# A planned attention-and-MLP kernel: head groups outermost in half of the blocks, gelu as one ScalarE batch, MLP work spread out, a new prologue

## The chip, the cores and the metric

The kernel runs on one core of a Trainium2 chip. A core has a matrix engine (TensorE, PE in the profile, with its weight loads as PEld), a vector engine (VectorE, DVE), an activation engine (ScalarE, ACT), a general engine (GpSimd, POOL) and a queue engine for transfers (SyncE, SP). Each works through its own instructions in order; they wait for each other by semaphores. On-chip data lies in SBUF, matmul results in PSUM, which has eight banks of 128 x 512 float32. The metric is the device time of one execution in microseconds.

## The reference, cut to what matters

Two branches share one normalised input, and their sum is added to `x` (2048 tokens, 512 columns).

```python
xn = layernorm(x)                                   # [1, 2048, 512]
# A: attention with 32 heads of 16 columns
qkv = xn @ wqkv;  scores = q @ k.T * 16 ** -0.5     # 32 x 2048 x 2048
a = softmax(scores) @ v;  A = a @ wo
# B: an MLP over the token axis
h = layernorm(xn)
u = gelu(einsum("bsd,sf->bdf", h, w1) + b1)         # tanh form; F = 1376
B = (einsum("bdf,fs->bds", u, w2) + b2).transpose(0, 2, 1)
out = x + A + B
```

The softmax needs 32 x 2048 x 2048 exponentials, about 134 million. They are what the kernel spends most instructions' time on.

## The kernel before, in words

**Tiling.** A block is one group of four heads (interleaved in the partitions) against 512 queries. There are 32 blocks: four query blocks `qb`, and in each eight head groups, named by `T` (0 to 3, a 128-column slice of Q, K and V) and `e_` (0 or 1). Each block has 16 key tiles and two half steps, so 32 *score tiles* of 128 x 1024, and the kernel has 1024 of them, numbered `n`. `blk_of` (L600) turns `n` into block, key tile, `qb`, `T` and `e_`. The query block is the outer loop, so all four slices `T` of K and V must be there within the first eight blocks (n up to 255).

**A score tile's way.** TensorE computes it with two matmuls (L616) into one of three *slots* of two PSUM banks. Then it takes one of two ways. Either ScalarE takes one exponential over 1024 columns (L640). Or VectorE builds a power of two from the bits: one pass from PSUM (L651, `dexp`) writes an int16 pattern that reads as a bfloat16, and three shifted copies of it (L656) are made on VectorE or GpSimd; the four together stand for one exponential. In both ways TensorE multiplies the result by V (L679, `pv`), once for a ScalarE tile, four times for a VectorE tile. V has a 17th column of constants, so the softmax's denominator comes out of the same matmuls. After a block, `task_epilogue` (L865) evacuates the sums (L870), divides and regroups them through small transfers (L907).

**Other work.** `task_qt`, `task_kt`, `task_vt` make the later slices of Q, K and V; `task_ut` makes one of 11 slices of u with 16 matmul steps, adds the bias (L804), and takes gelu by hand: two VectorE steps (L808, L810), a tanh on ScalarE (L812) and a last VectorE step (L814). It writes twice the gelu, and 0.5 at the end makes up for it. `task_fin` makes one of 16 output tiles: 11 steps with w2, then the attention's four steps with `wo`, then the evacuation (L854). All of them accumulate in one PSUM bank, `EX_BANK`, so only one runs at a time. GpSimd makes h from xn in the background (L478).

**Order.** Block 0 is written out by hand: two score tiles, two ScalarE exponentials, then a piece of the remaining prologue (`block0_work`, L594). VectorE takes no score tile there. From n = 32 on, a planner in the kernel's Python program (the `Sched` class and the loop behind L1113) keeps a modelled clock for each engine and appends, one at a time, whichever instruction it finds can start first. The chip only sees the resulting orders. The rules that matter here:

- a background task may start once `n` has reached its release number, and it goes ahead of other TensorE work when its due number comes near (L1017 to L1034);
- a score tile is issued when ScalarE will need one (L1197): `need = sc.free["act"] + EXP_I * ahead - 0.46 - DEAD_SLACK`, where `ahead` is the number of score tiles that wait to be taken. Up to that moment TensorE does `pv` or background work;
- VectorE takes a score tile if fewer than `D_FLY` = 3 of its tiles have shifts left to do and eight buffers are free (L1128).

**Prologue.** The loads of x go out on SP (six of them) and those of wqkv on ScalarE's queue (six). `pro_stage` (L558) pipelines statistics, normalisation, transposes and the first Q, K, V tiles over four token tiles. GpSimd computes one root per tile (L456, L458) behind several memsets (L375 to L400).

Of the kernel before, what the change touches and what calls it, by code (L numbers as in the profile page):

```python
# [9 lines left out]
BF16 = mybir.dt.bfloat16  # L10
# [18 lines left out]
GELU_C = 0.7978845608028654  # L29
GELU_A = 0.044715  # L30
# [16 lines left out]
NPRE = 4  # L47

# [15 lines left out]
D_STEAL = 0.8  # L64
P_KEEP = 4
DEAD_SLACK = 0.1
PORT_SLACK = 0.5
PE_FIT = 0.05

# [22 lines left out]
class Sched:  # L92
    ENGS = ("pe", "act", "dve", "pool", "sp")

    def __init__(self, nc, es):
        self.nc = nc
        self.es = es
        self.streams = {e: [] for e in self.ENGS}
        self.order = []
        self.last_writer = {}  # L100
        self.readers = {}
        self.dma_ops = []
        self.free = {e: 0.0 for e in self.ENGS}
        self.busy = {e: 0.0 for e in self.ENGS}
        self.pe_mode = None
        self.pe_end = 0.0
        self.pe_tiles = {}
        self.port_free = {"dve": 0.0, "pool": 0.0}
        self.port_op = None
# [32 lines left out]
    def _time(self, op, cost, ready, port):  # L142
# [7 lines left out]
        elif eng == "pe":  # L150
# [13 lines left out]
            op.t0, op.t1 = t, t + dur + PE_LAT - 0.214  # L164
        else:
# [4 lines left out]
        if port:  # L170
            self.port_free[eng] = op.t0 + cost[0]

# [106 lines left out]
def bass_parallel_sum__softmax_full_mha__mixer_token_mlp__prompt_kernel(  # L279
# [18 lines left out]
    with ExitStack() as es:  # L298
# [16 lines left out]
        gT_hi = sb("gT_hi", [128, NFT - 8, 512], BF16)  # L315
# [24 lines left out]
        u_sb = sb("u_sb", [128, 2, 512], F32)  # L340
        ga_sb = sb("ga_sb", [128, 2, 512], F32)
# [16 lines left out]
        def gT(ft):  # L358
            return wkv_raw[:, 512 * ft:512 * (ft + 1)] if ft < 8 else gT_hi[:, ft - 8, :]

        WKV_KEYS = [("wkv", j, T) for j in range(2) for T in range(4)]
        H_KEYS = [("xn", t) for t in range(NT)]

        def dma(q, dst, src, reads, writes, name="", noncontig=False, out_dma=False):
# [4 lines left out]
            else:  # L369
# [5 lines left out]
        sc.add("pool", lambda e: e.memset(ident[:], 0.0), writes=[("ident",)])  # L375
        sc.add("pool", lambda e: e.affine_select(ident[:], ident[:], [[-1, 128]], ALU.not_equal, 1.0,
                                                 base=0, channel_multiplier=1),
               reads=[("ident",)], writes=[("ident",)])
        sc.add("pool", lambda e: e.memset(mhalf[:], -0.5), writes=[("mhalf",)])
        sc.add("dve", lambda e: e.memset(b1c_bf[:], 0.0), writes=[("b1c",)])  # L380
# [7 lines left out]
        sc.add("dve", lambda e: e.memset(v17_main[:, :, 16:17], 0.5), writes=[("Vone",)], cost=(0.4, 0.5))  # L388
        sc.add("pool", lambda e: e.memset(qmask[:, 0:1], 0.0), writes=[("qmask",)])
        for r in range(4):  # L390
            sc.add("pool", lambda e, r=r: e.memset(qmask[32 * r:32 * r + 16, 0:1], QSCALE),
                   reads=[("qmask",)], writes=[("qmask",)])
        sc.add("pool", lambda e: e.tensor_scalar(qmask[:, 1:2], qmask[:, 0:1], -1.0, QSCALE, ALU.mult, ALU.add),
               reads=[("qmask",)], writes=[("qmask",)])
        for T in range(1, 4):
            sc.add("pool", lambda e, T=T: e.memset(vm_kh[:, :, 8 * T, 0:16], 0.0),
                   writes=[("VM", t, T) for t in range(NT)], cost=(0.3, 0.4))
        sc.add("pool", lambda e: e.memset(VM[:, NKT * H * 17:], 0.0), writes=[("VM", NKT, 0)], cost=(0.1, 0.2))
        sc.add("pool", lambda e: e.memset(QT[:, 2:4, :], 0.0), writes=[("QT", i, r) for i in (2, 3) for r in range(4)], cost=(0.9, 1.0))
        sc.add("pool", lambda e: e.memset(wo_t[:], 0.0), writes=[("wo_t", z) for z in range(4)], cost=(0.5, 0.6))  # L400

        def ld_x(a, b_):
            dma("sp", x_sb[:, a:b_, :],
# [3 lines left out]
        def ld_w(j, T0_, T1_):  # L407
# [7 lines left out]
            dma("act", dst, A_wqkv[:, c0:c1].rearrange("(ct p) n -> p ct n", p=128),  # L415
                reads=[], writes=keys, name="ld_wqkv")

        ld_w(2, 0, 1)
        ld_w(1, 0, 1)
        ld_w(0, 0, 1)  # L420
        ld_w(1, 1, 4)
        ld_w(2, 1, 4)
        ld_w(0, 1, 4)
        ld_x(0, 1)
        ld_x(1, 2)
        ld_x(2, 4)
        ld_x(4, 8)
        ld_x(8, 12)
        ld_x(12, 16)
# [7 lines left out]
        def late_consts():  # L437
            for e_ in range(2):
# [9 lines left out]
            sc.add("dve", lambda e: e.memset(gT_hi[FLAST:FLAST + 1, NFT - 9, :], 2.0), writes=[("gTone",)])  # L448


        def ln_stats(t):
# [4 lines left out]
            sc.add("pool", lambda e: e.tensor_scalar(mv[:, t, 3:4], mv[:, t, 1:2], EPS, None, ALU.add),  # L456
                   reads=[("mv", t)], writes=[("mv", t)], cost=(0.2, 0.28))
            sc.add("pool", lambda e: e.tensor_tensor(mv[:, t, 2:3], mv[:, t, 3:4], mhalf[:], ALU.pow),  # L458
                   reads=[("mv", t), ("mhalf",)], writes=[("mv", t)], cost=(0.5, 0.57))
# [28 lines left out]
        def transpose_pe(t, bk):  # L488
            for ct in range(NCT):
# [3 lines left out]
                    reads=[("xn", t), ("ident",)], writes=[("bank", bk)], cost=("F", (0, 1, 2, 3), 0.08))  # L493
# [6 lines left out]
        def kt_tile_pe(T, t, bk):  # L500
            j = t % 4
            for ct in range(NCT):
# [3 lines left out]
                    reads=[("wkv", 0, T), ("xnT", t)], writes=[("bank", bk)], cost=("F", (0, 1, 2, 3), 0.08))  # L506
# [6 lines left out]
        def vt_tile_pe(t, T, bk, j):  # L513
            for ct in range(NCT):
# [4 lines left out]
                    reads=[("wkv", 1, T), ("xnT", t)], writes=[("bank", bk)], cost=("F", (0, 1, 2, 3), 0.08))  # L519

        def vt_evac(tiles, T, bk, evac_eng):
# [5 lines left out]
                 cost=(0.25, 0.3) if n == 1 else None)  # L527
# [8 lines left out]
        def tb(t):  # L536
            return t % 2 if t < NPRE else 4

        def vb(t):
            return 2 + (t % 2) if t < NPRE else 5  # L540

        def kb(t):
            return PV_BANK if t < NPRE else EX_BANK

        def qt0_tile_pe(t):
            for ct in range(NCT):
                sc.add("pe", lambda e, ct=ct: e.matmul(
                    bank(EX_BANK)[:, 128 * t:128 * (t + 1)], lhsT=wq_sb[:, ct, 0:128],
                    rhs=xnT[:, ct, 128 * t:128 * (t + 1)], start=(ct == 0), stop=(ct == NCT - 1)),
                    reads=[("wq", 0), ("xnT", t)], writes=[("bank", EX_BANK)], cost=("F", (0, 1, 2, 3), 0.08))  # L550

        def qt0_evac():
            sc.add("act", lambda e: e.activation(QT[:, 0, :], bank(EX_BANK), ACTF.Identity, scale=qmask[:, 0:1]),
                   reads=[("bank", EX_BANK), ("qmask",)], writes=[("QT", 0, r) for r in range(4)], cost=(0.6, 0.69))
            sc.add("dve", lambda e: e.tensor_scalar(QT[:, 1, :], bank(EX_BANK), qmask[:, 1:2], None, ALU.mult),
                   reads=[("bank", EX_BANK), ("qmask",)], writes=[("QT", 1, r) for r in range(4)])

        def pro_stage(s_, pre):  # L558
            ev = "act" if pre else "dve"
            last = NPRE if pre else NT  # L560

            def ok(t):
                return (0 if pre else NPRE) <= t < last

            t = s_ - 5
            if ok(t):
                if t == NPRE - 1:
                    qt0_evac()
                kt_tile_evac(0, t, kb(t), "dve" if t >= NPRE else ("dve" if t % 2 == 0 else "act"))
                vt_evac([t], 0, vb(t), ev if t % 2 == 0 else "dve")  # L570
            t = s_ - 4
            if ok(t):
                kt_tile_pe(0, t, kb(t))
                if t < NPRE:
                    qt0_tile_pe(t)
                vt_tile_pe(t, 0, vb(t), 0)
            t = s_ - 3
            if ok(t):
                transpose_copy(t, tb(t), ev)
            t = s_ - 2  # L580
            if ok(t):
                transpose_pe(t, tb(t))
            t = s_
            if (0 if pre else NPRE + 2) <= t < (NPRE + 2 if pre else NT):
                ln_stats(t)
# [5 lines left out]
        for s_ in range(NSTG_PRE):  # L591
            pro_stage(s_, True)
# [792 lines left out]
```

## Time and profile before

Three runs took 734.94, 736.10 and 736.33 us; the median is 736.1. The profiled execution took 736.62 us and has a span of 734.8 us from its first to its last instruction, so 1.8 us lie outside of the span.

| engine | busy us | share of the span | instructions |
|---|---|---|---|
| PE | 686.5 | 93% | 12384 |
| ACT | 709.5 | 97% | 780 |
| DVE | 637.7 | 87% | 1060 |
| POOL | 350.1 | 48% | 390 |

Busy time is the union of an engine's instructions. Matmuls overlap each other and their ends are modelled, so a busy PE is not a PE at its peak. A group's mean duration contains a start and an end that the next instruction overlaps, so an engine's pace is a little faster than its mean durations; the starts of a row of instructions give the pace.

### The profile page before, as it was taken

How to read it: one execution, taken by the hardware profiler on the slowest of the kernel's cores; microseconds unless marked ns; L12 is line 12 of the kernel's file. 1: busy time of each engine (PE TensorE's matmuls, PEld its weight loads, DVE VectorE, ACT ScalarE, POOL GpSimd, SP SyncE). 2: the span in 40 equal slices, each digit the busy share in tenths (PEclk: the TensorE clock that was granted, in tenths of full speed). 3: DMA queues.
4: the chain of work that ended last, by engine and by line, in shares of the span. 5: the costliest groups of instructions: out<-in, count | busy, mean ns of one | idle time of the engine just before them, and what ended most of it. 6: DMA issues, size and time to landing. Idle time of an engine off the chain costs nothing.

```text
span 734.8 us, 28211 instructions
## 1 busy us (share of the span) xinstructions
PE 686.5 (93%) x12384; PEld 305.5 (42%) x12384; DVE 637.7 (87%) x1060; ACT 709.5 (97%) x780; POOL 350.1 (48%) x390
## 2 busy tenths in 40 slices
PE   4989999999999999999889999989989999999997
PEld 3434445444444444433334443433434444434442
DVE  6857788888898888898989999898999899989887
ACT  4899999999999999999999999998999999999995
POOL 5448455432433334445454544544555545645443
PEclk9899999999999999999999999997989999999999
DMA  7401000124232222220000212110000221221201
GB/s 201 94 2 25 18 9 21 25 59 89 44 70 62 41 66 59 57 49 18 22 21 20 52 37 67 38 32 12 20 17 18 49 49 39 50 50 41 46 22 44
DMA packets 85691, 32.25 MB, mean 44 GB/s; under 512 B 67392, under 2 KB 85568, under 8 KB 85568
## 3 DMA queue, kind: packets, MB, share of 16 engines
q1 hardware_dynamic: 82256, 28.74, 17.2%
q8 instruction: 97, 1.59, 0.9%
q10 hardware_dynamic: 3312, 1.70, 0.8%
q14 instruction: 26, 0.21, 0.1%
HBM read 21.76 MB, written 2.35 MB: 33 GB/s over the span
## 4 chain that ended last, share of the span: by engine, by line
ACT 77%; PE 15%; DVE 4%; DMA 1%; POOL 1%; issue 0%; SPq 0%; DVEq 0%
ACT pT L640 56%; ACT x_sb L640 21%; PE ps L616 5%; PE ps L679 5%; PE ps L709 4%; DVE pT L651 1%; DMA x_sb<-in_A_x_dram 1%; DMA wblk<-in_B_w_dram 1%; DVE pT L656 0%; DVE stats L452 0%; ACT ga_sb L812 0%; DVE x_sb L651 0%; POOL hx L478 0%; DVE x_sb L656 0%; DVE V L767 0%
## 5 line engine op out<-in xcount | busy, mean ns | idle before, releaser
L640 ACT ACTIVATE pT<-ps 128x1024 bf16<-128x1024 f32 x539 | 537.7, 1178 | 5.3 <-PE ps L616 5.1
L616 PE MATMUL ps<-QT,KT 32*128 32x512 bf16 x2048 | 285.3, 391 | 21.0 <-ACT pT L640 10.3
L651 DVE TENSOR_SCALAR pT<-ps 128x1024 int16<-128x1024 f32 x192 | 234.1, 1219 | 37.9 <-PE ps L616 36.9
L679 PE MATMUL ps<-pT,V 128*32 128x256 bf16 x4464 | 246.9, 281 | 6.1 <-DVE V L767 1.8
L640 ACT ACTIVATE x_sb<-ps 128x1024 bf16<-128x1024 f32 x219 | 240.9, 1171 | 2.3 <-PE ps L616 2.2
L656 POOL TENSOR_SCALAR pT<-pT 128x1024 int16<-128x1024 int16 x141 | 147.5, 1046 | 154.8 <-DVE pT L656 100.5
L616 PEld LDWEIGHTS ps<-QT,KT 32*128 32x128 bf16 x2048 | 79.2, 91 | 198.8 <-ACT pT L640 92.1
L679 PEld LDWEIGHTS ps<-pT,V 128*32 128x32 bf16 x4464 | 104.4, 96 | 110.3 <-issue 80.7
L679 PE MATMUL ps<-x_sb,V 128*32 128x256 bf16 x1760 | 115.3, 279 | 4.1 <-DVE OT L870 1.7
L656 DVE TENSOR_SCALAR pT<-pT 128x1024 int16<-128x1024 int16 x270 | 113.9, 443 | 2.7
L651 DVE TENSOR_SCALAR x_sb<-ps 128x1024 int16<-128x1024 f32 x74 | 90.1, 1218 | 12.4 <-PE ps L616 12.1
L656 POOL TENSOR_SCALAR x_sb<-pT 128x1024 int16<-128x1024 int16 x55 | 57.5, 1046 | 84.2 <-DVE pT L656 56.7
L656 POOL TENSOR_SCALAR pT<-x_sb 128x1024 int16<-128x1024 int16 x57 | 59.6, 1046 | 60.3 <-DVE pT L656 46.7
L679 PEld LDWEIGHTS ps<-x_sb,V 128*32 128x32 bf16 x1760 | 45.1, 96 | 41.8 <-issue 25.0
L679 PE MATMUL ps<-pT,VM 128*32 128x256 bf16 x764 | 55.2, 278 | 0.3 <-POOL VM L531 0.3
L709 PE MATMUL ps<-hx,wblk 128*32 128x512 bf16 x688 | 53.7, 381 | 1.5 <-DVE Qall L731 0.8
L656 DVE TENSOR_SCALAR x_sb<-pT 128x1024 int16<-128x1024 int16 x110 | 48.6, 446 | 1.1
L656 DVE TENSOR_SCALAR pT<-x_sb 128x1024 int16<-128x1024 int16 x108 | 43.9, 434 | 1.1
L709 PE MATMUL ps<-wkv_raw,wblk 128*32 128x512 bf16 x512 | 43.0, 381 | 1.8 <-DMA wblk<-in_B_w_dram 1.2
L907 POOL TENSOR_TENSOR oT<-oC,denb 128x256 bf16<-128x256 f32 (+1 forms) x32 | 23.3, 728 | 27.9 <-DVE pT L656 14.5
L679 PEld LDWEIGHTS ps<-pT,VM 128*32 128x32 bf16 x764 | 20.5, 97 | 9.0 <-issue 2.7
L656 POOL TENSOR_SCALAR x_sb<-x_sb 128x1024 int16<-128x1024 int16 x17 | 17.8, 1046 | 13.3 <-DVE pT L656 11.6
(89 smaller groups left out, 438.1 us busy)
## 6 DMA issues: line engine op xcount, KB each, us to landing
wblk<-in_B_w_dram SPq DMA_DIRECT2D x10, 512.0 KB, 4.6
wblk<-in_B_w_dram SPq DMA_DIRECT2D x16, 320.0 KB, 3.8
oC<-OT SPq DMA_DIRECT2D x248, 16.0 KB, 1.8
denb<-rden_scratch SPq DMA_DIRECT2D x124, 32.0 KB, 1.9
xr<-in_A_x_dram SPq DMA_DIRECT2D x16, 128.0 KB, 2.4
dcomp<-OT SPq DMA_DIRECT2D x124, 2.0 KB, 1.7
QT<-Qall SPq DMA_DIRECT2D x120, 16.0 KB, 1.8
out_dram<-osb SPq DMA_DIRECT2D x14, 128.0 KB, 1.9
```

The costliest lines, as they stand in the source:

```text
L616: specs.append(dict(eng="pe", fn=lambda e, r=r, bk=bk: e.matmul(bank(bk), lhsT=KT[32 * r:32 * r + 32, T, 128 * kt:128 * (kt + 1)], rhs=QT[ ...
L640: return [dict(eng="act", fn=lambda e: e.activation(buf(pbuf[n]), ps[:, s_ * 1024:(s_ + 1) * 1024], ACTF.Exp, scale=LN2_128), reads=[("ban ...
L651: return dict(eng="dve", fn=lambda e: e.tensor_scalar(buf_i(w), ps[:, s_ * 1024:(s_ + 1) * 1024], IBIAS, 0.0, ALU.add, ALU.max), reads=[(" ...
L656: return dict(eng=eng, fn=lambda e: e.tensor_scalar(buf_i(o), buf_i(w), float(SHIFTS[k]), 1.0, ALU.add, ALU.mult), reads=[("pT", w)], writ ...
L679: specs.append(dict(eng="pe", fn=lambda e, c=c, h=h, i=i, off=off: e.matmul(bank(PV_BANK)[32 * c:32 * c + 32, 256 * par:256 * par + 256], ...
L709: specs.append(dict(eng="pe", fn=lambda e, c=c, w=w: e.matmul(bank(EX_BANK)[32 * c:32 * c + w, :], lhsT=lhs_of(32 * c, 32 * c + w), rhs=rh ...
L907: yield "pool", [dict(eng="pool", fn=lambda e, cs=cs: e.tensor_tensor(oT[0:m, qb % 2, T, cs], oC32[0:m, tb_, cs], denb[0:m, tb_, cs], ALU. ...
```

## The change

It has these parts.

1. **Order of blocks.** A list `PAIRS` puts `T` outermost for the query blocks 0 and 1 (the first 16 blocks) and keeps the query block outermost for 2 and 3. A slice of K and V is now needed every four blocks instead of every two.
2. **Due numbers.** K and V tasks become due at n = 40, 170 and 236, 14 apart; the 11 u tasks at n = 100 to 480, 38 apart (before at 184 to 314, 13 apart, and only after the last K and V task); the output tasks from 500, 650, 800 and 920 on, 24 to 32 apart.
3. **Gelu.** A u task only adds the bias into a bfloat16 tile. When all 11 are done, six ScalarE instructions take gelu in place, five over 1024 columns and one over 512. Factors 0.5 and 2.0 elsewhere become 1.0.
4. **Score tiles for VectorE.** `need` is now taken from a sorted list that also has the time at which VectorE will be free, if it may take a tile.
5. **`fill`.** Where the modelled TensorE activity of the last 3.42 us is at most 0.5 and no background task is open, matmuls without use are put into the modelled idle time.
6. **Prologue.** The first four x tiles are loaded one by one on two queues, ahead of all weights; ScalarE takes the sums for tile 1; the first roots come ahead of most memsets; the four tiles are transposed together; Q and K come first and V moves into block 0; matmuls without use run at the start, in three steps of block 0 and in the tail.

```diff
+D_LATE = 0.6
+ACT_WIN = 3.42
+ACT_MIN = 0.5
...
+    def pe_activity(self, t):
+        s = 0.0
+        for t0, w in reversed(self.pe_log):
+            if t0 < t - ACT_WIN:
+                break
+            s += w
+        return s / ACT_WIN
...
-        ld_w(2, 0, 1)
...
-        ld_x(0, 1)
...
+        ld_x("sp", 0, 1)
+        ld_x("act", 1, 2)
+        ld_x("sp", 2, 3)
+        ld_x("act", 3, 4)
+        for j in (1, 0, 2):
+            ld_w(j, 0, 1)
+        ld_x("sp", 4, 6)
...
+        def ln_sums(t):
+            for fn, col in ((ACTF.Identity, 3), (ACTF.Square, 1)):
+                sc.add("act", lambda e, fn=fn, col=col: e.activation(xn_sb[:, t, :], x_sb[:, t, :], fn,
+                                                                    accum_out=mv[:, t, col:col + 1]),
...
+        def warm_up(n, bk, src=pT[:, NPB - 1, 0:512], keys=(("pT", NPB - 1),)):
+            for _ in range(n):
+                sc.add("pe", lambda e: e.matmul(bank(bk), lhsT=src[:, 0:128], rhs=src, start=True, stop=True),
...
+        sc.add("act", lambda e: e.activation(rcomp[:, 0, 0:1], mhalf[:], ACTF.Exp), reads=[("mhalf",)],
+        ln_sums(1)
+        warm_up(N_WARM, 5)
+        ln_stats(0)
...
+        ln_moments(1)
+        ln_rstd(1, 2)
+        ln_stats(3)
+        for t in range(NPRE):
+            ln_norm(t)
+        late_memsets()
+        for t in range(NPRE):
+            transpose_pe(t, TB[t])
+        for t in range(NPRE):
+            transpose_copy(t, TB[t], "dve" if t == 2 else "act")
...
+            if period == 1:
+                warm_up(5, PV_BANK, KT[:, 0, 0:512], [("KTt", 0, z) for z in range(4)])
+            if period >= NKT - 2:
+                warm_up(3, 4, KT[:, 0, 0:512], [("KTt", 0, z) for z in range(4)])
...
+        PAIRS = [(qb, T) for T in range(4) for qb in (0, 1)] + [(qb, T) for qb in (2, 3) for T in range(4)]
...
         def blk_of(n):
-            qb, G = divmod(b, NG)
-            T, e_ = divmod(G, 2)
+            p, e_ = divmod(b, 2)
+            qb, T = PAIRS[p]
...
-            yield "dve", [dict(eng="dve", fn=lambda e: e.scalar_tensor_tensor(ga, u, GELU_A, u, ALU.mult, ALU.mult),
...
+        def task_gelu():
+            parts = [(gT_sb[:, f:f + 2, :], (f, f + 1)) for f in range(0, NFT - 1, 2)]
+            parts += [(gT_sb[0:FLAST, NFT - 1, :], (NFT - 1,))]
+            yield "gate", lambda: len(u_done) == NFT
+            yield "act", [dict(eng="act", fn=lambda e, ap=ap: e.activation(ap, ap, ACTF.Gelu_apprx_tanh),
...
-        KV_DUE = {1: BN + 2, 2: 2 * BN + 16, 3: 3 * BN + 24}
+        KV_DUE = {1: BN + 8, 2: 170, 3: 236}
...
-        UT0, UT_STEP = 4 * BN + 16, 13
+            due = UT_DUE + UT_STEP * i
+            ext_tasks.append((due - UT_LEAD, due, "ut", task_ut(i), ("ut", i)))
...
+            due = FIN_DUE[st // 4] + FIN_STEP[st // 4] * (st % 4)
...
+        def fill(t_next, same):
+            if cur_ext is not None or last_n is None or sc.pe_activity(t_next) > ACT_MIN:
+                return
...
+            for _ in range(int((t_next - sc.pe_end - 2 * PE_SWITCH - 0.1) / 0.22)):
+                sc.add("pe", lambda e: e.matmul(bank(EX_BANK), lhsT=ident[:], rhs=wo_c[:, 0, :], start=True, stop=True),
...
-                need = sc.free["act"] + EXP_I * ahead - 0.46 - DEAD_SLACK
+                wants = [sc.free["act"] + EXP_I * i for i in range(4)]
+                if fly < D_FLY and len(free_p) >= 4 + P_KEEP:
+                    wants.append(sc.free["dve"] + backlog(sc.free["dve"]) + D_LATE)
+                need = sorted(wants)[ahead] - 0.46 - DEAD_SLACK
```

More of the change, by code (lines that the diff above doesn't have):

```diff
@@ L47 @@
 NPRE = 4
+N_WARM = 11
 SEM = 0.05
@@ L358, in gT @@
         def gT(ft):
[L359 to L361 removed]
+            return gT_sb[:, ft, :]
         H_KEYS = [("xn", t) for t in range(NT)]
@@ L437, in late_consts @@
         def late_consts():
+            sc.add("pool", lambda e: e.memset(wo_t[:], 0.0), writes=[("wo_t", z) for z in range(4)], cost=(1.75, 1.8))
             for e_ in range(2):
```

325 lines of the change are left out of this document (179 added, 146 removed).

## The prediction

> **What bounds the kernel now.** I read the page's chain of waits first, then the chain in order of time for ScalarE's pace.
>
> ```profile
> ACT 77%; PE 15%; DVE 4%; DMA 1%; POOL 1%; issue 0%; SPq 0%; DVEq 0%
> ```
>
> ```profile
> 313.06 11.92 ACT pT L640 x13
> ```
>
> ScalarE's exponentials set the end; 13 of them in a row take 11.92 us, 0.917 us each. The table of stretches cuts the span into block 0, the planned stage after it (first line below), and parts of that stage. The second table counts the score tiles that VectorE took (L651).
>
> ```profile
> 48.12:726.46 678.34, 647.59 (x11976) 284.59 (x11972) 601.43 (x955) 673.08 (x738) 324.83 (x330) 0.98 0.17 39
> ```
>
> ```profile
> 15.69:48.12 32.43, 28.41 (x325) 14.15 (x325) 22.89 (x69) 30.42 (x32) 13.91 (x29) 0.87 0.27 55
> 48.12:140.00 91.88, 87.47 (x2090) 43.23 (x2090) 74.37 (x113) 90.63 (x100) 52.33 (x60) 0.99 0.08 17
> 140.00:320.00 180.00, 176.39 (x3199) 77.18 (x3190) 157.19 (x248) 179.40 (x201) 68.13 (x69) 1.00 0.27 60
> ```
>
> ```profile
> 48.12:140.00 91.88, 32.92 (x27) 0.99 0.08 17
> 140.00:320.00 180.00, 73.06 (x60) 1.00 0.27 60
> 320.00:496.00 176.00, 95.16 (x79) 1.00 0.15 34
> 551.00:726.46 175.46, 93.86 (x77) 0.99 0.17 40
> 48.12:726.46 678.34, 324.25 (x266) 0.98 0.17 39
> ```
>
> The columns after the length are busy times of PE, PEld, DVE, ACT and POOL, then the granted clock. In the planned stage ScalarE is busy for 673.08 of 678.34 us: it has 5.3 us to win by waiting less. It can only get shorter by giving tiles away. Of the stage's 992 tiles VectorE takes 266 and ScalarE 726, and 726 x 0.917 = 666 us. So **each tile more on VectorE is worth 0.917 us**, and the question is how many more VectorE can take. VectorE is idle for 678.3 - 601.4 = 77 us there. It took 27 tiles in 92 us and 60 in 180 us while K, V and u were made (0.29 and 0.33 a microsecond), but 79 in 176 and 77 in 175 later (0.45 and 0.44), the last of these with eight output tasks beside them. The two early parts are the loose ones, with 17.5 (91.9 - 74.4) and 22.8 of the 77 idle us in them.
>
> **What a tile costs VectorE.** The order of time on VectorE, in a stretch without waits:
>
> ```profile
> 315.38 1.22 DVE L651 TENSOR_SCALAR pT<-ps 128x1024 int16<-128x1024 f32 x1
> 316.52 0.75 DVE L656 TENSOR_SCALAR pT<-pT 128x1024 int16<-128x1024 int16 x2
> 317.19 1.22 DVE L651 TENSOR_SCALAR x_sb<-ps 128x1024 int16<-128x1024 f32 x1
> ...
> 319.32 0.24 DVE L885 RECIPROCAL rcomp<-dcomp 128x16 f32<-128x16 f32 x1
> ```
>
> With two shifts on VectorE and one on GpSimd a tile takes 317.19 - 315.38 = 1.81 us, with all three on VectorE (left out above) 319.32 - 317.19 = 2.13. GpSimd waits for VectorE's shifts already, so I take 2.1 for an additional tile; bounds 1.81 and 2.13.
>
> **Gelu, VectorE's side.** These steps go; the bias step stays.
>
> ```profile
> L810 DVE SCALAR_TENSOR_TENSOR ga_sb<-ga_sb,u_sb 128x512 f32<-128x512 f32 (+1 forms) x11 | 7.6, 692 | 0.4
> L808 DVE SCALAR_TENSOR_TENSOR ga_sb<-u_sb 128x512 f32<-128x512 f32 (+1 forms) x11 | 7.5, 685 | 0.2
> L814 DVE SCALAR_TENSOR_TENSOR wkv_raw<-ga_sb,u_sb 128x512 bf16<-128x512 f32 x8 | 5.5, 690 | 3.0 <-ACT ga_sb L812 2.9
> L814 DVE SCALAR_TENSOR_TENSOR gT_hi<-ga_sb,u_sb 128x512 bf16<-128x512 f32 (+1 forms) x3 | 2.0, 683 | 0.0
> ```
>
> 7.6 + 7.5 + 5.5 + 2.0 = 22.6 us of VectorE are freed, all in a stage in which VectorE is short.
>
> **Gelu, ScalarE's side.** A tanh followed by an exponential, and the only table load of the trace:
>
> ```profile
> 156.73 0.85 ACT L812 ACTIVATE ga_sb<-ga_sb 128x512 f32<-128x512 f32 x1
> 157.25 2.17 ACT L640 ACTIVATE pT<-ps 128x1024 bf16<-128x1024 f32 x2
> ```
>
> ```profile
> L484 ACT ACT_TABLE_LOAD x1 | 1.3, 1283 | 4.1 <-issue 4.1
> ```
>
> A tanh holds ScalarE for 157.25 - 156.73 = 0.52 us; eleven go, 5.7 us. Gelu of 1024 columns is not in the trace; the nearest row is the exponential of the same width, 0.917 us, and the narrow one is like the tanh. Five and one make 4.6 + 0.5 = 5.1 us, and going to another table and back is two loads, 2.6 us, if gelu is in another table than exp and tanh. Together 7.7 - 5.7 = **2.0 us more** on ScalarE; without loads it would be -0.6. Behind the six stand exponentials, which the three slots hold; TensorE goes on with V products and VectorE with tiles, so nothing else is late for long.
> The Trainium skill (ScalarE: Activation LUTs, What ACT_TABLE_LOAD costs) gives a load the same 1283 ns, which the row has, and adds a drain of about 1380 ns to each switch, which no run here shows yet. By it two switches are 5.3 us instead of 2.6, and the forecast below would be 2 us higher.
>
> **Clock.** One of the stretches with a halved TensorE clock, in steps of 2 us:
>
> ```profile
> 496.00:498.00 2.00, 1.25 (x10) 0.30 (x6) 2.00 (x5) 2.00 (x4) 0.73 (x1) 0.79 0.00 0
> ...
> 504.00:506.00 2.00, 2.00 (x30) 0.62 (x22) 1.33 (x3) 1.33 (x2) 0.58 (x1) 0.50 0.11 23
> ```
>
> TensorE had little to do, then got half its clock (0.50), and ScalarE ran dry (1.33 of 2.00). `fill` puts matmuls into such stretches. Of ScalarE's 5.3 idle us I give back 3, bounds 0 and 5.3; the added matmuls take time that the model holds to be idle, so I cost them at nothing, and what they cost where the model errs is the last rival. So ScalarE's fixed work changes by 2.0 - 3.0 = -1.0 us, bounds +2.0 and -3.3.
>
> **Score tiles for VectorE, and the spreading.** The waits:
>
> ```profile
> PEld ps L616 <- ACT pT L640: 92.1, 287, 0.8
> ...
> DVE pT L651 <- PE ps L616: 36.9, 45, 3.0
> ...
> DVE x_sb L651 <- PE ps L616: 12.1, 11, 3.4
> ```
>
> VectorE stood for 49 us with nothing to do but wait for a score tile, since the rule looked at ScalarE alone. The new rule and the spread tasks work on the same wait. They can win back none of it (no slot free: TensorE itself waits 92 us for ScalarE to leave slots) or all of it. I take half, 24.5 us. The order of blocks costs no work: as many K, V and Q tasks and transfers as before, only later. Ahead of them in SP's queue nothing new is put.
>
> **The sum for the planned stage.** VectorE gains 22.6 + 24.5 = 47.1 us, but a stage shorter by s takes 0.887 s of busy time from it (601.4 / 678.3). With d tiles moved, d = (47.1 - 0.887 s) / 2.1 and s = 0.917 d + 1.0. That gives s = 15.6 and d = 16. As a cross-check, VectorE at its later 0.44 during the first 272 us would take 120 tiles instead of 87: 33 more, twice my d, and possible only if K, V and u cost nothing.
>
> **Prologue.** The order of time before the first exponential, and block 0 on ScalarE:
>
> ```profile
> 4.15 1.80 POOL L400 MEMSET wo_t<- 128x2048 bf16 x1
> ...
> 6.03 0.23 POOL L456 TENSOR_SCALAR mv<-mv 128x1 f32<-128x1 f32 x1
> ...
> 10.70 0.41 DVE L462 TENSOR_SCALAR hx<-x_sb,mv 128x512 bf16<-128x512 bf16 x1
> ...
> 15.69 2.99 ACT L640 ACTIVATE pT<-ps 128x1024 bf16<-128x1024 f32 x3 [0.32 <-PE ps L616]
> ```
>
> ```profile
> 25.27 22.85 ACT L640 ACTIVATE pT<-ps 128x1024 bf16<-128x1024 f32 x24 [0.55 <-PE ps L616]
> ```
>
> The first root waited for memsets until 6.03; the fourth tile was normalised at 11.1, and 4.6 us later the first exponential began. Without the memsets in front and with x loaded first I put the fourth normalisation at 7.6 (statistics and roots of four tiles in 3.5 us from 3.1 on, a 0.41 norm behind), and the rest, with Q and K ahead of V, at 3.0 instead of 4.6: first exponential at 10.6, **5.1 us earlier**; bounds 3 and 6. Block 0 took 32.43 us for 32 exponentials, while the 24 from 25.27 on ran at 22.85 / 24 = 0.952; all 32 at that pace are 30.5, **2.0 us less**, if its useless matmuls keep the clock up; bounds 1 and 2.5. The tail keeps its steps.
>
> **Forecast.** The profiled execution took 736.6 (its span 734.8 and 1.8 around it): 736.6 - 15.6 - 7.1 = 713.9. The runs' median lies 0.5 below it, so I say **713 us**. With a quarter or three quarters of the 49 us won, s is 11.6 or 19.5, and with the prologue's bounds this case reaches from 708 to 720.
>
> **Rivals.**
> *The wait goes almost entirely* (all 49 us, 1.81 a tile, ScalarE -3.3): d = (71.6 - 0.887 s) / 1.81 gives s = 27, and with 8 us from the prologue 701. For it: 0.45 tiles a microsecond were reached beside output tasks. Against: VectorE's evacuations of K, V and u remain.
> *The rule finds no slot* (none of the 49, 2.13 a tile, ScalarE +2.0): s = 5.6, with 4 us from the prologue 726. For it: the 92 us above.
> *The change doesn't reach the chip*, since VectorE's eight buffers and three tiles in flight limit it and the prologue's transfers are late all the same: about 736.
> *The score tile for VectorE, or a useless matmul, makes ScalarE late.* TensorE works in order, so one put ahead holds back whatever ScalarE needs next. The one such late start ahead of the 24 exponentials above cost 0.55 us. There would be about 282 VectorE tiles; the gains of 22.7 are eaten from 0.08 us of delay for each. If one in five costs 0.55, the loss is 31 us, and the time 744: slower. Against it: ScalarE idles only 5.3 us in the stage now, with TensorE busy for 95% of it.
> The Trainium skill (TensorE: Matmul & The Clock Gate, Part 1: The HAM clock gate) says that the clock halves after an idle window of about 3.4 us. [...] The gelu batch is itself 7.7 us in which ScalarE frees no slot; by that rule it could add one such episode, some 2 us by three such rows as that at 504, inside the first case's range.
>
> **Chances.** First case 0.45, wait gone 0.20, no slot 0.20, no effect 0.05, ScalarE late 0.10. Under 0.2% (1.5 us) a measurement can't tell a change from none. Faster 0.85, same 0.05, slower 0.10. The range 698 to 729 leaves out the last two cases and a little of the second.
>
> **What would show it.** First exponential near 10.6 us; VectorE with some 282 tiles, more of them before 320 us; its wait for L616 near 25 us; six gelu instructions and two table loads in one stretch of under 8 us; no granted clock of 0.50 behind block 0; ScalarE idle below 3 us in the planned stage. I am wrong if VectorE's tiles stay at 266, or if ScalarE's idle time ahead of L640 grows by tens of microseconds.

## The result, and the profile after

The changed kernel takes 714.0 us (median of four runs, 713.6 to 714.4), against 736.2 before: a ratio of 0.970 with a 95% interval of 0.968 to 0.972. Its profiled execution has a span of 712.3 us. The forecast was 713. That the sum came out so close is partly luck: the planned stage won 2.9 us more than forecast (18.5 against 15.6), the start and block 0 together 1.3 us less (5.8 against 7.1), and the tail lost 1.8 us that the sum did not have.

The page's head and its slices of TensorE's granted clock:

```profile
span 712.3 us, 28991 instructions
...
PE 686.4 (96%) x12711; PEld 308.7 (43%) x12716; DVE 666.9 (94%) x1093; ACT 690.6 (97%) x752; POOL 384.1 (54%) x420
...
PEclk9999999999999999999999999999999999999999
```

The stretches, cut as before: up to the first exponential, block 0, the planned stage up to the end of the last exponential, and the tail. The columns are those of the prediction's tables.

```profile
0.00:11.43 11.43, 8.61 (x65) 4.39 (x66) 7.69 (x26) 5.09 (x11) 7.93 (x26) 1.00 0.84 252
11.43:42.34 30.91, 28.11 (x349) 14.52 (x350) 23.91 (x69) 30.06 (x32) 15.32 (x33) 1.00 0.19 46
42.34:702.19 659.85, 643.51 (x12254) 287.23 (x12256) 629.10 (x987) 654.89 (x710) 359.28 (x360) 1.00 0.19 42
702.19:712.30 10.11, 6.20 (x57) 2.60 (x50) 6.16 (x14) 0.60 (x2) 1.53 (x3) 1.00 0.17 55
```

Against 15.69, 32.43, 678.34 and 8.34 us before, these are 4.3, 1.5 and 18.5 us less, and 1.8 us more in the tail. VectorE's score tiles (L726 now) by stage, and its wait for score tiles:

```profile
42.34:140.00 97.66, 47.43 (x39) 1.00 0.20 41
140.00:320.00 180.00, 92.00 (x76) 1.00 0.19 39
320.00:496.00 176.00, 97.90 (x82) 1.00 0.19 44
...
42.34:702.19 659.85, 353.42 (x291) 1.00 0.19 42
```

```profile
DVE pT L726 <- PE ps L691: 9.2, 21, 2.3
...
DVE x_sb L726 <- PE ps L691: 6.3, 11, 3.2
```

VectorE took 291 tiles, 25 more than before; 39 in 98 us and 76 in 180 us are 0.40 and 0.42 a microsecond where 0.29 and 0.33 had been. Its wait for score tiles fell from 49.0 to 15.5 us, its idle time in the planned stage from 77 to 31.

The chain of work that ended last, 77% ScalarE before the change, now runs through three engines:

```profile
PE 40%; ACT 34%; DVE 19%; issue 2%; SPq 2%; DMA 1%; POOL 1%; DVEq 0%; POOLq 0%; ACTq 0%
```

In the planned stage TensorE is busy for 98% of the time now, VectorE for 95% and ScalarE for 99%.

The gelu batch on ScalarE, in order of time:

```profile
350.55 1.02 ACT L715 ACTIVATE x_sb<-ps 128x1024 bf16<-128x1024 f32 x1 [0.46 <-PE ps L691]
351.59 1.28 ACT L888 ACT_TABLE_LOAD   x1
352.88 5.37 ACT L888 ACTIVATE gT_sb<-gT_sb 128x1024 bf16<-128x1024 bf16 x6
358.27 1.28 ACT L715 ACT_TABLE_LOAD   x1
359.56 1.94 ACT L715 ACTIVATE x_sb<-ps 128x1024 bf16<-128x1024 f32 x2
```

It holds ScalarE for 359.56 - 351.57 = 8.0 us, two table loads included. The granted clock stays at 1.00 through it. Each load starts 0.02 us or less behind the instruction ahead of it and is followed within 0.01 us; only the ending instruction's last tenth of a microsecond is no longer overlapped. The Trainium skill (ScalarE: Activation LUTs, What ACT_TABLE_LOAD costs) gives a drain of about 1380 ns for each switch beside the load. In this trace it does not come on top.

### The profile page after: what moved, and what is told of

Same layout as the page of the kernel before. It is cut to its first block, busy times and chain, and to the rows that moved or that the text cites. A ratio compares the mean times of both kernels' runs of the same rounds, so it can differ in the third digit from the quotient of the medians.

```text
span 712.3 us, 28991 instructions
## 1 busy us (share of the span) xinstructions
PE 686.4 (96%) x12711; PEld 308.7 (43%) x12716; DVE 666.9 (94%) x1093; ACT 690.6 (97%) x752; POOL 384.1 (54%) x420
## 3 DMA queue, kind: packets, MB, share of 16 engines
q1 hardware_dynamic: 85168, 30.05, 18.5%
## 4 chain that ended last, share of the span: by engine, by line
PE 40%; ACT 34%; DVE 19%; issue 2%; SPq 2%; DMA 1%; POOL 1%; DVEq 0%; POOLq 0%; ACTq 0%
ACT pT L715 24%; PE ps L691 14%; PE ps L754 14%; PE ps L784 9%; ACT x_sb L715 8%; DVE pT L726 8%; DVE pT L731 5%; DVE x_sb L726 2%; DVE x_sb L731 2%; SPq L388 2%; PE ps L833 1%; ACT gT_sb L888 1%; DVE OT L944 1%; PE ps L597 1%; DMA denb<-rden_scratch 0%
## 5 line engine op out<-in xcount | busy, mean ns | idle before, releaser
L715 ACT ACTIVATE pT<-ps 128x1024 bf16<-128x1024 f32 x522 | 511.8, 1113 | 4.3 <-PE ps L691 2.9
L726 DVE TENSOR_SCALAR pT<-ps 128x1024 int16<-128x1024 f32 x201 | 244.1, 1215 | 10.1 <-PE ps L691 9.2
L715 ACT ACTIVATE x_sb<-ps 128x1024 bf16<-128x1024 f32 x211 | 225.0, 1120 | 1.9 <-PE ps L691 1.7
L731 POOL TENSOR_SCALAR pT<-pT 128x1024 int16<-128x1024 int16 x149 | 156.3, 1049 | 124.0 <-DVE pT L731 82.1
L731 DVE TENSOR_SCALAR pT<-pT 128x1024 int16<-128x1024 int16 x284 | 122.2, 452 | 3.2
L726 DVE TENSOR_SCALAR x_sb<-ps 128x1024 int16<-128x1024 f32 x90 | 109.4, 1215 | 6.5 <-PE ps L691 6.3
L731 POOL TENSOR_SCALAR pT<-x_sb 128x1024 int16<-128x1024 int16 x73 | 76.3, 1045 | 62.2 <-DVE pT L731 47.4
L754 PE MATMUL ps<-pT,VM 128*32 128x256 bf16 x864 | 61.4, 275 | 1.2 <-POOL VM L569 1.2
L731 DVE TENSOR_SCALAR pT<-x_sb 128x1024 int16<-128x1024 int16 x131 | 57.9, 465 | 1.5
L784 PE MATMUL ps<-gT_sb,wblk 128*32 128x512 bf16 (+1 forms) x704 | 58.4, 384 | 0.6 <-DVE Qall L806 0.6
```

What stands on the lines that cost most here:

```text
L715: return [dict(eng="act", fn=lambda e: e.activation(buf(pbuf[n]), ps[:, s_ * 1024:(s_ + 1) * 1024], ACTF.Exp, scale=LN2_128), reads=[("ban ...
L726: return dict(eng="dve", fn=lambda e: e.tensor_scalar(buf_i(w), ps[:, s_ * 1024:(s_ + 1) * 1024], IBIAS, 0.0, ALU.add, ALU.max), reads=[(" ...
L731: return dict(eng=eng, fn=lambda e: e.tensor_scalar(buf_i(o), buf_i(w), float(SHIFTS[k]), 1.0, ALU.add, ALU.mult), reads=[("pT", w)], writ ...
L754: specs.append(dict(eng="pe", fn=lambda e, c=c, h=h, i=i, off=off: e.matmul(bank(PV_BANK)[32 * c:32 * c + 32, 256 * par:256 * par + 256], ...
L784: specs.append(dict(eng="pe", fn=lambda e, c=c, w=w: e.matmul(bank(EX_BANK)[32 * c:32 * c + w, :], lhsT=lhs_of(32 * c, 32 * c + w), rhs=rh ...
```

## The experiments

One account serves all of them. In the planned stage ScalarE has 992 score tiles less those of VectorE, at 0.917 us each. What is left of the stage's length is gelu on ScalarE (5.7 us by hand, 8.0 as a batch) and a remainder, which I call ScalarE's late starts. As a remainder it makes the account come out by construction. Two readings of the traces stand beside it: the median step from one exponential's start to the next is 0.904 us in every one of these kernels, so the pace is the same in all; and ScalarE's idle time in the stage, the last column, is largest where the late starts are. It is smaller than they are: the records of two exponentials overlap (1.02 us long and 0.92 us apart in the rows above), so a start can be late without idle time. The lengths come from each kernel's own profiled execution, from the first exponential behind block 0 to the end of the last.

| kernel | median us | planned stage | VectorE tiles | rest beside 0.917 us a tile | of it late starts | ScalarE idle |
|---|---|---|---|---|---|---|
| before | 736.2 | 678.1 | 266 | 12.4 | 6.7 | 5.0 |
| prologue_only | 735.5 | 682.2 | 265 | 15.6 | 9.9 | 7.3 |
| spread_only | 726.3 | 671.4 | 269 | 8.4 | 2.7 | 1.6 |
| need_old | 722.4 | 669.6 | 275 | 12.1 | 4.1 | 2.8 |
| gelu_hand | 719.6 | 663.6 | 281 | 11.7 | 6.0 | 2.7 |
| order_old | 713.8 | 659.3 | 291 | 16.5 | 8.5 | 4.6 |
| after | 714.0 | 659.9 | 291 | 17.0 | 9.0 | 5.0 |
| need_alone | 744.9 | 682.9 | 287 | 36.4 | 30.7 | 25.3 |
| ut_packed | 749.0 | 690.5 | 291 | 47.7 | 39.7 | 35.1 |
| best_a | 707.0 | 653.5 | 293 | 12.5 | 4.5 | 2.3 |

For instance after: 659.9 - 0.917 x (992 - 291) = 17.0, less 8.0 of gelu.

### The old rule for score tiles

```diff
-                    wants.append(sc.free["dve"] + backlog(sc.free["dve"]) + D_LATE)
+                    pass
...
-            if cur_ext is not None or last_n is None or ...
+            if fin_next >= NT or cur_ext is not None or last_n is None or ...
```

The second edit keeps `fill` out of the bank in which the last output task waits.

> The changed kernel (714.0 us, 291 score tiles on VectorE, VectorE's wait for score tiles 15.5 us, first exponential at 11.4) with the old rule for score tiles: only ScalarE's need counts. The program then has 275 VectorE tiles, 16 fewer. Theory A (each tile moved to VectorE is worth 0.917 us, and the rule is what feeds VectorE): ScalarE has 16 x 0.917 = 14.7 us more to do, less some 3 us that it now starts late: about 726 us, VectorE's wait for score tiles 30 us or more. Theory B (the spread work did it, and what the rule gives, ScalarE's late starts take back): 714 to 717 us.

Measured: 722.4 us (721.4 to 723.6), 8.4 more than the changed kernel, with 16 tiles fewer on VectorE and these waits:

```profile
DVE pT L726 <- PE ps L691: 32.1, 42, 2.3
DVE x_sb L726 <- PE ps L691: 19.4, 23, 3.2
```

The wait of 51.5 us is back, as large as before the change. So spreading does nothing to it; the rule does. Theory A holds in kind. Its 726 is too high, since ScalarE starts 4.9 us less late and the tail is 1.1 us shorter without the rule: of 14.7 us that the tiles are worth, some 6 are handed back.

### Gelu by hand

```diff
-            yield "ev", [... tensor_scalar(gT(ft)[0:m, :], bank(EX_BANK)[0:m, :], b1col[0:m, ft:ft + 1], None, ALU.add) ...]
-            yield "call", lambda: u_done.append(ft)
...
+            yield "ev", [... tensor_scalar(u, bank(EX_BANK)[0:m, :], b1col[0:m, ft:ft + 1], 0.5, ALU.add, ALU.mult) ...]
+            yield "dve", [... scalar_tensor_tensor(ga, u, 4 * 0.044715, u, ALU.mult, ALU.mult) ...]
+            yield "dve", [... scalar_tensor_tensor(ga, ga, 1.0, u, ALU.add, ALU.mult) ...]
+            yield "act", [... activation(ga, ga, ACTF.Tanh, scale=2 * 0.7978845608028654) ...]
+            yield "dve", [... scalar_tensor_tensor(u, ga, 1.0, u, ALU.add, ALU.mult) ...]
```

> The changed kernel with gelu by hand again, slice by slice: three VectorE steps and a tanh on ScalarE for each of the 11 u tasks (in bfloat16, with a scratch that is free at that time), no batch. The program has 281 VectorE tiles, 10 fewer. Theory A: ScalarE gets 10 x 0.917 = 9.2 us more, and 8.1 us of batch with its two table loads become 5.7 us of tanh: 714.0 + 9.2 - 2.4 = 721 us. Theory B (the batch's hole costs what VectorE gains): 713 to 716 us.

Measured: 719.6 us (718.5 to 723.1), 5.6 more, with 281 tiles, as theory A has it. The three VectorE steps by hand are these rows; in bfloat16 they are no shorter than the 0.69 us of the float32 ones:

```profile
L883 DVE SCALAR_TENSOR_TENSOR osb<-gT_sb 128x512 bf16<-128x512 bf16 (+1 forms) x11 | 8.7, 792 | 0.2
...
L889 DVE SCALAR_TENSOR_TENSOR gT_sb<-osb,gT_sb 128x512 bf16<-128x512 bf16 (+1 forms) x11 | 8.0, 729 | 1.1 <-ACT osb L887 1.1
L885 DVE SCALAR_TENSOR_TENSOR osb<-osb,gT_sb 128x512 bf16<-128x512 bf16 (+1 forms) x11 | 7.6, 687 | 0.3
```

### The old order of blocks

```diff
-        PAIRS = [(qb, T) for T in range(4) for qb in (0, 1)] + [(qb, T) for qb in (2, 3) for T in range(4)]
+        PAIRS = [(qb, T) for qb in range(4) for T in range(4)]
...
-        KV_DUE = {1: BN + 8, 2: 170, 3: 236}
+        KV_DUE = {1: BN + 2, 2: 2 * BN + 16, 3: 3 * BN + 24}
...
-                ext_tasks.append((KV_DUE[T] - 8, KV_DUE[T] + KV_STEP * c, "kt", task_kt(T, c), None))
+                ext_tasks.append((BN * max(0, T - 1), KV_DUE[T] + 6 * c, "kt", task_kt(T, c), None))
...
```

The line of the V tasks is changed in the same way.

> The changed kernel with the query block outermost everywhere and the K and V tasks due as before (all by about n = 140); the u and output tasks stay spread. The program has 291 VectorE tiles like the changed kernel. Theory A (time goes by the number of VectorE tiles; the order of blocks is only a means to spread work): 714 us within 1.5. Theory B (without the new order K and V crowd the start, score tiles come late to both engines): 718 to 722 us, with fewer VectorE tiles before 140 us and idle ScalarE there.

Measured: 713.8 us (712.4 to 714.8), the same as the changed kernel, with the same 291 tiles. The part that stands first in the change's title has no effect that can be measured here, beside the other parts. In this run K and V crowd the first 140 us at no cost, while the u tasks stay spread.

### The new prologue alone

The changed kernel with all of the planned stage's parts undone: the edits of the three experiments above, the old due numbers of Q, u and output tasks, and no fill.

> The kernel before with only the new prologue (block 0 and tail of the changed kernel too): old order of blocks, old due numbers, gelu by hand slice by slice, old rule for score tiles, no fill. 265 VectorE tiles, against 266 before. Theory A: what the first 48 us lose (first exponential 15.7 to 11.4, block 0 32.4 to 30.9 us, 5.8 us together) stays won to the end: 736.2 - 5.8 = 730.4, within 2 us. Theory B (the gain is lost again where K and V are waited for): 734 us or more.

Measured: 735.5 us (732.6 to 736.3, ten runs), a ratio of 0.9986 to before, interval 0.9972 to 1.0001, so that it can't be told from no change: theory B. Block 0 ends 4.9 us earlier (43.5 in place of 48.4), and the planned stage is 4.1 us longer. These 20 us stretches lie among the u tasks (granted clock third from the right):

```profile
240.00:260.00 20.00, 18.88 (x316) 8.43 (x312) 17.67 (x29) 18.98 (x22) 7.30 (x7) 0.93 0.24 57
260.00:280.00 20.00, 19.96 (x330) 8.09 (x326) 16.52 (x28) 18.56 (x21) 8.84 (x9) 0.90 0.18 41
```

ScalarE is busy for 18.98 and 18.56 us in them, where the kernel before had 20.00 and 19.40 at a clock of 1.00. In all it starts 3.2 us later than before, and one tile fewer is on VectorE (0.9 us): together the 4.1. Why the clock fell just there isn't settled; the planner's order differs from before in details all along the stage.

### The spread tasks, without rule and batch

The edits of the first two experiments together. One part of what is left isn't in the list of the change: a Q task is now due 54 numbers ahead of its block in place of 20 (`Q_LEAD`). The spread tasks below include it.

> The changed kernel with both the old rule for score tiles and gelu by hand; new prologue, new order of blocks and spread due numbers stay. 269 VectorE tiles. Theory A (the parts add up): 714.0 + 8.4 (rule) + 5.6 (gelu) = 728 us, so that prologue and spreading together are worth 8 us of 22. Theory B (rule and batch only pay together): 722 to 724 us. Theory C (prologue and spreading are worth nothing without them): 734 us or more.

Measured: 726.3 us (724.9 to 727.5): between A and B, and nearer to A. Against prologue_only it is 9.2 us faster with four tiles more, worth 3.7 us; ScalarE's late starts fall from 9.9 to 2.7 us. The planned stage, in one row:

```profile
43.81:715.19 671.38, 646.80 (x12037) 288.92 (x12033) 602.91 (x955) 669.82 (x735) 338.94 (x341) 1.00 0.18 41
```

ScalarE is idle for 1.6 of 671.4 us, at a clock of 1.00 throughout. So with the spread tasks ScalarE starts less late and the clock stays up, and VectorE hardly gains. Which of them does it, the u tasks further apart or the earlier Q tasks, and what the clock has to do with it, no run separates.

### The rule alone, on the kernel before

```diff
-                need = sc.free["act"] + EXP_I * ahead - 0.46 - DEAD_SLACK
+                wants = [sc.free["act"] + EXP_I * i for i in range(4)]
+                if fly < D_FLY and len(free_p) >= 4 + P_KEEP:
+                    wants.append(sc.free["dve"] + backlog(sc.free["dve"]) + D_LATE)
+                need = sorted(wants)[ahead] - 0.46 - DEAD_SLACK
```

> The kernel before (736.2 us, 266 VectorE tiles) with only the new rule for score tiles. The program has 287 VectorE tiles, 21 more. Theory A (each is worth 0.917 us): some 15 to 19 us faster, 717 to 721 us. Theory B (without spread work the tile for VectorE comes at the cost of ScalarE's, or of V products that wait): 730 us or more, with ScalarE's idle time ahead of its exponentials at 20 us or more against 7.6 before.

Measured: 744.9 us (741.5 to 748.0), ratio 1.014, interval 1.010 to 1.018: 1.4% longer, with 21 more tiles on VectorE. They save 19.3 us of exponentials, and ScalarE's late starts grow by 24.0 us. The largest group of them, in the order of time on ScalarE and then on TensorE:

```profile
208.38 1.11 ACT L641 ACTIVATE pT<-ps 128x1024 bf16<-128x1024 f32 x1
213.74 0.63 ACT L813 ACTIVATE ga_sb<-ga_sb 128x512 f32<-128x512 f32 x1 [4.25 <-DVE ga_sb L811]
215.88 1.02 ACT L641 ACTIVATE pT<-ps 128x1024 bf16<-128x1024 f32 x1 [1.51 <-PE ps L617]
218.59 2.86 ACT L641 ACTIVATE pT<-ps 128x1024 bf16<-128x1024 f32 x3 [1.69 <-PE ps L617]
```

```profile
205.78 1.05 PE L710 MATMUL ps<-xnT,wq_sb 128*32 128x512 bf16 x16
...
207.81 3.64 PE L710 MATMUL ps<-hx,wblk 128*32 128x512 bf16 x64
...
212.31 3.21 PE L710 MATMUL ps<-hx,wblk 128*32 128x512 bf16 x56
...
218.17 0.39 PE L617 MATMUL ps<-QT,KT 32*128 32x512 bf16 x3 [1.47 <-DMA QT<-Qall]
```

The Q task of the next pair of blocks is computed only at 205.8 us, behind u tasks in the one bank. Its eight transfers (`QT<-Qall`) go out on SP's queue between 207.8 and 218.1 us, with others of that queue among them, and the last lands by 218.2. Until then TensorE does u work and hardly a score tile, and ScalarE runs dry for over 7 us. With more tiles on VectorE the score tiles of a block are used up sooner, and Q comes too late. TensorE's waits for `QT<-Qall`, weight loads included, are 5.0 us in all here, 0.4 in the changed kernel and none before the change. This group is 7.5 of the 25.3 us that ScalarE idles. Another 4.8 us lie at 117 to 124 us, behind K and V tasks and one more wait for Q, and 3.9 at 264 to 268, behind a u task without one; the rest was not traced. That late Q tasks are the cause is shown for the first group, and not for the whole.

### The u tasks crowded

```diff
-UT_DUE, UT_STEP = 100, 38
+UT_DUE, UT_STEP = 184, 13
```

> The changed kernel (714.0 us) with the 11 u tasks due close together again (184 to 314, 13 apart, in place of 100 to 480, 38 apart); all else is the changed kernel's, 291 VectorE tiles. Theory A (time goes by the number of VectorE tiles): 714 us within 2. Theory B (spreading is the carrier: crowded background work delays the Q tasks and V products that score tiles wait for, so that both engines run out of tiles): 730 us or more, with over 15 us of idle ScalarE between 150 and 330 us.

Measured: 749.0 us (746.0 to 751.5), ratio 1.018, interval 1.014 to 1.022, with the changed kernel's 291 tiles, as theory B has it. One gap carries most of it:

```profile
ACT x_sb L715 <- PE ps L691: 28.4, 6, 27.4
```

ScalarE waits 27.4 us in one piece, up to 266.0 us, while TensorE goes through u, K, Q and V tasks one after the other. The Q tasks are due 54 numbers ahead here too, and this one is reached at 257.3 us, so an early due number alone doesn't keep Q in time. In this kernel K and V come later than in the kernel before, so u meets them; it shows what the spread due numbers avoid, and not what the kernel before suffered.

### The useless matmuls made tiny

```diff
-                sc.add("pe", lambda e: e.matmul(bank(bk), lhsT=src[:, 0:128], rhs=src, start=True, stop=True),
+                sc.add("pe", lambda e: e.matmul(bank(bk)[:, 0:16], lhsT=src[:, 0:128], rhs=src[:, 0:16], start=True, stop=True),
```

and the same for the two kinds of fill.

> The changed kernel with its 28 useless warm-up matmuls and 6 fill matmuls cut to 16 columns: the same orders and waits on every engine, nearly no TensorE activity from them. Theory A (they keep the TensorE clock up where it matters): a clock of 0.50 in the prologue and in block 0, as before the change, first exponential 1 us later, block 0 near 33 us, 717 to 718 us. Theory B (the spread work keeps TensorE busy without them): behind block 0 the clock stays at 1.00, and the time is 714 to 715.5 us.

Measured: 715.2 us (715.0 to 720.0), as theory B has it. The planned stage stays at 1.00, and block 0 takes 30.7 us at a clock of 0.98:

```profile
11.98:42.68 30.70, 27.05 (x351) 14.10 (x350) 23.98 (x69) 30.01 (x32) 15.39 (x33) 0.98 0.17 40
```

So the useless matmuls are not what shortened block 0. `fill` itself put six matmuls into the whole program, so it isn't what keeps the clock up later. Nor do the useless matmuls at the start hold the clock there in every execution. The same changed kernel had two clocks in the stretch before the first exponential, in the execution above and in the one of the next section (first and second line):

```profile
10.00:12.00 2.00, 1.90 (x33) 1.50 (x30) 1.40 (x4) 1.05 (x2) 0.69 (x2) 1.00 1.10 355
10.00:12.00 2.00, 2.00 (x21) 2.00 (x20) 0.70 (x2) 0.47 (x1) 0.79 (x2) 0.50 1.10 338
```

The first exponential started at 11.4 us in the one and at 13.0 in the other. With the tiny matmuls the clock was 1.00 and the start at 12.0; over the twelve profiled executions with the new prologue it lies between 11.3 and 13.0.

### The tail, and two better versions

```diff
-                    if n % BN > D_LAST or (qi == 0 and ...
+                    if n % BN > D_LAST or n >= NN - 2 or (qi == 0 and ...
```

> The changed kernel once more, beside the next three on the same chip: 714.0 us within 1, 291 VectorE tiles, tail (from the last exponential's end to the end) 10.1 us against 8.3 before.

> The changed kernel, but VectorE may not take one of the last two score tiles (290 VectorE tiles). Theory A (the longer tail comes from VectorE's last tile, whose shifts start when ScalarE is done): the tail goes back to about 8.4 us and ScalarE takes one tile more, 0.9 us, so that the time is 713 us. Theory B (the tail is long for another reason, such as its six added matmuls): the tail stays at 10 us or more and the time at 714 to 715.

Measured on one chip: 715.2 us (714.2 to 715.7) and 714.0 (713.1 to 716.4). In the changed kernel VectorE's last tile and its shifts, and the first step of the tail behind them:

```profile
701.08 1.22 DVE L726 TENSOR_SCALAR pT<-ps 128x1024 int16<-128x1024 f32 x1
702.33 0.43 DVE L731 TENSOR_SCALAR pT<-pT 128x1024 int16<-128x1024 int16 x1
...
703.15 0.76 DVE L731 TENSOR_SCALAR pT<-pT 128x1024 int16<-128x1024 int16 x2
704.31 0.72 DVE L1008 STREAM_TRANSPOSE denb<-ps 128x512 f32<-128x512 f32 x1 [0.40 <-PE ps L754]
```

ScalarE was done at 702.2, but the shifts run to 703.9. With the limit the tail is back to 8.3 us:

```profile
703.97:712.30 8.33, 4.99 (x25) 2.13 (x26) 4.59 (x9) 0.60 (x2) 1.44 (x2) 1.00 0.19 63
```

Theory A holds for the tail. ScalarE's extra tile and a later end of the planned stage take most of it back; whether the whole is faster these runs can't tell.

Two further versions keep the limit and the old order of blocks, and change margins. This is the first one's; the second's stand in its expectation:

```diff
-D_BACK = 0.5
-D_STEAL = 0.8
-D_LATE = 0.6
+D_BACK = 0.8
+D_STEAL = 0.9
+D_LATE = 0.7
...
-Q_LEAD = 54
-UT_DUE, UT_STEP = 100, 38
-UT_LEAD = 16
+Q_LEAD = 60
+UT_DUE, UT_STEP = 104, 36
+UT_LEAD = 12
```

> A version meant to beat both: the old order of blocks, the new rule with other margins (VectorE counted as late by 0.7 in place of 0.6 us, a backlog of 0.8 in place of 0.5 us allowed, 0.9 in place of 0.8 us of lead over ScalarE), u tasks at 104 + 36 i, Q tasks 60 in place of 54 numbers ahead, no VectorE tile among the last two. 293 VectorE tiles. Theory A (tiles and ScalarE's late starts are all that counts): 2 tiles more are 1.8 us, the tail gives 1.7, late starts 3 less: 707 to 710 us. Theory B (the chip's own small delays, which a plan doesn't hold, eat such gains): 712 to 715 us.

> The same aim with other margins: old order of blocks, a backlog of 0.7 us allowed, u tasks at 100 + 36 i released 24 ahead, Q tasks 60 ahead, no VectorE tile among the last two. 296 VectorE tiles. Theory A: 5 tiles more are 4.6 us, the tail gives 1.7: 707 to 710 us. Theory B: ScalarE's late starts grow with the tiles as they did in the changed kernel, 712 to 715 us.

Measured: 707.0 us (705.7 to 708.7), ratio to before 0.961, interval 0.957 to 0.964; and 708.0 (707.2 to 708.9), 0.962, 0.959 to 0.965. Both beat both kernels, and both lie in the range of their theory A. The planned stage and tail of the first:

```profile
43.60:697.08 653.48, 642.40 (x12300) 289.00 (x12299) 624.85 (x991) 651.18 (x708) 367.50 (x370) 1.00 0.19 42
697.08:705.40 8.32, 5.04 (x29) 2.13 (x26) 4.60 (x9) 0.60 (x1) 0.53 (x1) 0.96 0.20 65
```

Two tiles more give 1.8 us, the tail 1.8, and 4.5 us come from ScalarE starting less late. The second has 296 tiles, the most of all, and late starts of 7.6 us, and is no faster. Its tail is 9.6 us in spite of the limit, where 1.7 us had been expected back: TensorE still has V products to do until 699.1 us, 1.7 us after the last exponential. So VectorE's last tile is one way to a long tail, and not the only one.

## Why the prediction was right, and where it wasn't

- **The bound.** Right as to what a tile is worth, and incomplete. Tiles taken from ScalarE do shorten the end, at a pace that is the same in every kernel; but ScalarE's late starts had no term of their own in my sum, and in the changed kernel the chain that ended last lies 40% on TensorE and 34% on ScalarE. The sum charges TensorE nothing for a tile on VectorE, though it multiplies V four times instead of once. The two traces have 7288 and 7588 such matmuls, 12 more for each of the 25 tiles. Groups of four start 0.11 us apart in the changed kernel (701.34, 701.45, 701.56 us), so these are some 8 us of TensorE, an estimate from those starts. Its idle time in the planned stage fell from 31 to 16 us. How much of the late starts comes from that isn't shown.
- **Score tiles for VectorE.** The term was mis-sized: I took 24.5 us of wait as won, and 33.5 were, and 25 tiles moved in place of 16. The wait alone doesn't give 25: with it and the measured 18.3 us my formula has (22.6 + 33.5 - 0.887 x 18.3) / 2.1 = 19. VectorE's other idle time in the stage, which the formula only lets shrink with the stage, fell from 28 to 15 us, and a tile cost 2.0 us and not 2.1 (27.7 us more busy time and 22.6 freed, for 25 tiles). Then ScalarE's fixed work grew where I had it shrink by 1.0: 0.917 x 25 - 2.3 (gelu) - 2.3 (late starts, 6.7 to 9.0) = 18.3 us (678.1 to 659.9, rounded), against 15.6 forecast. Two errors, 9 tiles more and 5.6 us of fixed work more, work against each other here.
- **The 92 us** on which the rival without a free slot rested were misread. That row is one of weight loads (PEld), and not of a TensorE that stands: it was busy for 647.6 of the stage's 678.3 us. In the changed kernel the same row is nearly as long, while VectorE's wait is down to 15.5 us:

```profile
PEld ps L691 <- ACT pT L715: 89.6, 310, 0.8
```

- **That rule and spreading are one term** was the wrong step. I wrote that "The new rule and the spread tasks work on the same wait". They don't: the spread tasks without the rule leave the wait at 51.5 us and go with 7.2 us less of late starts, and the rule alone cuts the wait to 16.9 us and makes the kernel slower. Of the two schedules tried, it pays only in the one that spreads TensorE's other work and has the Q tasks ahead.
- **Gelu.** ScalarE's 7.7 us were right in size (8.0 measured), and VectorE's 22.6 fit the 24.3 us that the three steps take by hand in bfloat16; the batch is worth 5.6 us of the whole. The clock episode that I feared behind the batch didn't come.
- **Clock.** The clock did go to 1.00, but not by `fill`. Of ScalarE's idle time 3 us were to come back, and in the changed kernel they did not: 5.3 us before, 5.0 after. With the spread tasks alone it is 1.6, so it came back there, and was spent again with the rule and the batch together. No run changes the clock alone, so what it is worth by itself stays open. My reading that TensorE lost its clock for want of work isn't shown either: its longest idle stretch between 494 and 509 us of the kernel before is 0.45 us, and from 502 to 506 us it was busy throughout at 0.50.
- **Prologue.** 4.3 and 1.5 us were measured at their place, 5.1 and 2.0 forecast. The terms that I gave for the fourth normalisation add up to 3.1 + 3.5 + 0.41 = 7.0 us and not to the 7.6 that I wrote; it ended at 8.7, since the four stand in a row behind the last statistics (6.5 us) and take 2.2 us. The 4.3 is one of the better executions; the other one of the same kernel won 2.7. The condition on block 0, that useless matmuls keep the clock up, was wrong. And "7.1" as a term that carries to the end was wrong as a step: alone the prologue gave 0.7 us, which can't be told from none. In the sum it counts only since the spread stage behind it doesn't give the time back.
- **Tail.** Costed at nothing, it grew by 1.8 us, because VectorE, now fed to the end, holds the last tile; without that tile it is 8.3 us again.
- **The slower rival** ("The score tile for VectorE, or a useless matmul, makes ScalarE late") was right in kind and happened in need_alone. In the largest group of gaps the mechanism is another than the one named: not a tile put ahead of ScalarE's, but a Q task that sits behind u tasks. In the changed kernel the delay is (9.0 - 6.7) / 291 = 0.008 us a tile, far below the 0.08 at which it would decide.

## What to carry to other kernels

Feeding a helper engine better makes the main stream consume its inputs faster, so look at everything with a fixed place in the order (here the Q tasks) and see whether it has to move ahead as well; the same rule was worth 8.4 us of gain in one schedule, and cost 8.5 in another. Account for a stage as count x pace of the bounding engine, plus its late starts: two kernels with the same count differed by 31 us in the second term alone. Then read the chain again: an engine with little idle time left, as TensorE here, can be the next bound. And a gain at the start is worth nothing until one has seen that the stage behind it ends earlier by as much.

## What the runs showed of the hardware

A switch of ScalarE's table and back cost two loads of 1.28 us and next to nothing beside (8.0 us with six gelu instructions of 5.37 us in all). TensorE's granted clock fell to 0.50 at 498 us of the kernel before, with no idle stretch over 0.45 us around it, and at 10 to 12 us it was 1.00 in one execution of the changed kernel and 0.50 in another. VectorE's steps of the gelu by hand, with two operands in SBUF, took 0.69 to 0.79 us in bfloat16, no less than the 0.69 us that they took in float32.
